# Expert scores of a PEER layer by seven block products: from three quads of expert tiles and six pairs of row blocks to four quads and seven pairs

## The chip, the cores and the metric

The kernel runs on one core of a Trainium2 chip. The metric is the device time of the program in microseconds (us), the median of three runs. The core has a matrix engine (PE), a vector engine (DVE, VectorE), an activation engine (ACT, ScalarE), a general engine (POOL, GpSimd) and queues that start transfers (nearly all of them SP's, SyncE's). Each engine takes its own instructions strictly in order and waits at semaphores for the others, so what is queued behind a waiting instruction waits too.

## The reference

x has 2048 rows of 512 numbers. Three things are added: x itself, the real part of a two-dimensional Fourier transform of the normalised x, and a PEER expert layer with 32 heads, 64 x 64 = 4096 experts and 2 experts chosen per head.

```python
xn = _layernorm(x, axis=-1)
# FNet: a = xn @ Cd^T, b = xn @ Sd^T; y = Cs @ a - Ss @ b
# PEER, with q1, q2 = halves of xn @ w_q[h] and K = 2:
s1 = jnp.einsum("nhd,ed->nhe", q1, k1)
s2 = jnp.einsum("nhd,ed->nhe", q2, k2)
i1 = jnp.argsort(-s1, axis=-1)[..., :K]
i2 = jnp.argsort(-s2, axis=-1)[..., :K]
# the four sums t1 + t2, the best two of them: scores top_s, experts top_e
g = _softmax(top_s, axis=-1)
act = _gelu(jnp.einsum("nd,nhkd->nhk", xf, u[top_e]))
out = jnp.einsum("nhk,nhk,nhkd->nd", g, act, v[top_e])
return x + _A_ref(...) + out
```

## The kernel before, in words

The 2048 rows are 16 row blocks of 128. The 4096 experts are 16 groups of 256. `u_sb[g]` and `v_sb[g]` hold the weights of group g as two f16 numbers each, a high and a low part, and a product of two such pairs is three f16 matmuls (high by high, high by low, low by high).

**Up to 78 us** the kernel normalises x and prepares the Fourier matrices and the folded query-key matrices.

**78 to 418 us, the scores.** Eight chunks j of four heads run over 16 row tiles i; a slot is one (j, i), counted n = 16 j + i. PE computes the scores of a tile (`s_mm`, line 252, 12 matmuls) into one of four PSUM buffers, ACT copies them to one of four SBUF buffers (line 952), and VectorE finds the largest values (MAX8, line 956) and their places (FIND_INDEX8, line 960). After each chunk `routing` turns these into the softmax weights g and the expert numbers, in parts that are queued at slots i = 1, 2 and 4 of the next chunk. It goes to and fro between POOL (lines 885 to 887, 890, 896, 902 and on) and VectorE (lines 888, 889, 894, 895, then the CAST of line 897 and the subtraction of line 898). In the same stretch a hand-written list `todo[n]` hangs other work behind the slots:

- `fill_uv(which, g)`: scales the weights of a group, splits them into high and low (ACT lines 780 and 781, POOL line 782). A table `slots` says where: the u tiles 0, 1, 2 and 3 come at slots 29, 31, 36 and 45.
- `sum_u(g, part)`: for a group that belongs to a quad, part 0 makes four sums of quadrants of the u tile (POOL lines 809 to 812) in a scratch that lies in a v tile not yet filled, called at the end of `fill_uv`; parts 1 and 2 five slots after the fill split them into high and low (`split4`: ACT line 794, POOL line 795) and store them to `s_d` in HBM.
- `sum_x(b, part)`: the same for a pair of row blocks (POOL lines 823, 824 and 829 to 832, then `split4` and a store to `t_d`).
- `m_prep` (POOL line 167, 2 operations a call) and `stage_v` (POOL line 852) prepare other weights.

**418 to 1103 us, the phases.** For each row block b a z phase computes x times u for all 4096 experts and takes gelu of it, and a v phase multiplies the weighted activations by v. The z phases come for two row blocks at once, with two v phases between them, but for blocks 0, 1, 14 and 15, which have single ones. Two ways of doing z exist:

- `u_part` (matmuls on line 1095): the plain product. For a pair of blocks a call is one expert group, 24 matmuls of 256 columns; for one block it is two groups, 48 matmuls of 128 columns.
- `z_pair` with `slot` (matmuls on line 1168): Winograd's seven products in place of eight for a 2 x 2 block matrix, over a *quad* of four expert groups and a pair of row blocks. A slot is one of the seven products, 24 matmuls of 128 columns. Products 1, 2 and 4 read u tiles as they are; 5, 6, 7 and 3 read sums, which `ring_load` (line 1151) brings from `s_d` into a ring of three tiles of 512 KB. After its matmuls a slot hands its PSUM bank to ACT (a copy or gelu) and VectorE (an addition, lines 1204, 1212 and 1216).

In each z pair of before, groups 4 to 15 go in three quads (21 slots), and groups 0 to 3 are plain calls ("c" in the string `SEQ`, which writes the order out by hand).

Beside z and v run, for each row block: `g_mm(b, k)`, k = 0 to 3 (VectorE builds one-hot tiles L and R on lines 1246, 1251 and 1254 in a ring of three; 32 matmuls on line 1256); `w_part(b, k)` (VectorE line 1264, ACT line 1271, VectorE line 1272), which multiplies the activations by these weights; and single units of a comparison of the given Fourier matrices with those that the kernel makes itself (`compare`: VectorE lines 1332, 1338, 1340, 1351 and 1357, ACT line 1377, with loads of 448 KB; `fit`: ACT). A table built with `put(phase, place, ...)` says behind which eighth of a v phase or sixteenth of a z pair each of them is issued: G, W, `compact_d`, U for `compare`, F for `fit`. The v tiles of groups 9 to 15 do not stay on chip and come from `v_d` by transfers of 512 KB.

## Time and profile before

| | |
|---|---|
| median of three runs | 1132.64 us (1132.04 to 1133.97) |
| the profiled execution | 1132.17 us, of which the span that the trace covers is 1130.4 us |
| busy in the span | PE 1114.2, weight loads 724.4, DVE 960.3, ACT 657.5, POOL 319.4 us |
| granted PE clock, mean | 0.998 |
| scores | 78 to 417.7 us |
| phases z(0), z(1), v(0) | 417.7 to 488.7 us |
| phases from z(2, 3) on | 488.7 to 1103 us |

The table is read so: an engine that is busy for nearly the whole span is the one whose work sets the time, unless much of what it does there is waiting under another name. Lines such as L1168 are those of the kernel before.

### The profile page before, as it was taken

The numbers are of one execution on the slowest core, as the hardware profiler recorded it, in microseconds if no ns is written. First come the engines' busy times: TensorE is split into PE (matmuls) and PEld (weight loads), VectorE is DVE, ScalarE is ACT, GpSimd is POOL, SyncE is SP. The second block draws the span as 40 slices with busy tenths as digits, with TensorE's granted clock in tenths as the row PEclk, the third lists the DMA queues.
The fourth block names the chain that finished last, engine by engine and source line by source line (L and its number), as shares of the span: only waits on it lengthen the run. The fifth ranks groups of instructions, "written<-read, shape, count | busy, mean of one in ns | idle before, by whom it ended". The sixth has DMA issues, their size and how long they took to land.

```text
span 1130.4 us, 28284 instructions
## 1 busy us (share of the span) xinstructions
PE 1114.2 (99%) x11180; PEld 724.4 (64%) x11180; DVE 960.3 (85%) x2873; ACT 657.5 (58%) x1099; POOL 319.4 (28%) x357
## 2 busy tenths in 40 slices
...
GB/s 274 289 207 171 162 168 197 112 154 190 105 187 103 104 50 190 157 249 143 258 216 184 239 206 199 235 218 187 226 199 215 227 199 225 190 246 167 239 150 106
DMA packets 122540, 213.10 MB, mean 189 GB/s; under 512 B 34580, under 2 KB 62107, under 8 KB 122398
## 3 DMA queue, kind: packets, MB, share of 16 engines
...
HBM read 178.34 MB, written 27.07 MB: 182 GB/s over the span
## 4 chain that ended last, share of the span: by engine, by line
PE 50%; DVE 10%; DMA 3%; ACT 2%; POOL 2%; issue 1%; SPq 0%; DVEq 0%; ACTq 0%; POOLq 0%
PE v L1301 24%; PE z L1168 13%; PE z L1095 10%; PE g L1256 4%; DMA cx<-in_cb_dram 3%; DVE L L1246 2%; DVE vals L956 1%; DVE idx L960 1%; DVE w L1264 1%; DVE act L1272 1%; DVE cx L1351 1%; DVE R L1251 0%; DMA fit<-in_wq_dram 0%; DVE cx L1340 0%; POOL v L824 0%
## 5 line engine op out<-in xcount | busy, mean ns | idle before, releaser
L252 PE MATMUL s<-m,xq 128*128 128x512 f16 x1344 | 297.4, 379 | 1.0 <-ACT ss L952 0.5
L1301 PE MATMUL v<-v,act 128*128 128x512 f16 x1056 | 233.4, 379 | 1.0 <-DMA v<-v_d 1.0
L252 PEld LDWEIGHTS <-xq 128*128 128x128 f16 x1344 | 129.8, 98 | 152.2 <-issue 2.4
L1314 POOL TENSOR_TENSOR y<-y,xr 128x512 f32<-128x512 f32 x15 | 26.1, 1740 | 623.4 <-DMA y<-y_d 383.7
L1246 DVE TENSOR_TENSOR L<-io_lam,cmp 128x2048 f16<-128x2048 f16 x128 | 157.5, 1230 | 26.9 <-PE g L1256 26.8
L1301 PEld LDWEIGHTS <-act 128*128 128x128 f16 x1056 | 101.2, 98 | 118.7 <-issue 1.3
L1095 PE MATMUL z<-xb,u 128*128 128x128 f16 (+1 forms) x2112 | 154.3, 234 | 0.1
L1095 PEld LDWEIGHTS <-u 128*128 128x128 f16 x2112 | 141.4, 98 | 6.6 <-issue 0.2
L956 DVE MAX8 vals<-ss 128x8 f32<-128x64 f32 x896 | 133.5, 216 | 5.6 <-ACT ss L952 5.6
L1301 PE MATMUL v<-v,w 128*128 128x512 f16 x480 | 106.3, 379 | 0.1
L952 ACT ACTIVATE ss<-s,wsc 128x512 f32<-128x512 f32 x120 | 81.4, 682 | 41.2 <-PE s L252 35.1
L1377 ACT ACTIVATE cx<-cx 128x896 f32<-128x896 f32 x64 | 60.4, 944 | 72.6 <-DVE cx L1357 53.2
L1168 PEld LDWEIGHTS <-s 128*128 128x128 f16 x1656 | 94.8, 98 | 0.1
L960 DVE FIND_INDEX8 idx<-vals,ss 128x8 uint16<-128x256 f32 x224 | 93.8, 419 | 0.0
L1271 ACT ACTIVATE act<-w 128x1024 f16<-128x1024 f32 x36 | 48.3, 1357 | 68.3 <-DVE w L1264 68.0
L1301 PEld LDWEIGHTS <-w 128*128 128x128 f16 x480 | 45.9, 98 | 53.6 <-issue 0.4
L1168 PE MATMUL z<-x,s 128*128 128x128 f16 x1248 | 78.1, 219 | 0.0
L1168 PEld LDWEIGHTS <-u 128*128 128x128 f16 x1296 | 74.9, 98 | 1.8 <-issue 1.4
L1256 PEld LDWEIGHTS <-L 128*128 128x128 f16 x2048 | 60.3, 96 | 12.7 <-issue 2.1
L1351 DVE TENSOR_TENSOR cx<-cx 128x512 f32<-128x512 f32 (+2 forms) x84 | 48.4, 613 | 23.5 <-DMA cx<-in_cb_dram 23.5
L1264 DVE SCALAR_TENSOR_TENSOR w<-act,scl,g 128x1024 f32<-128x1024 f32 x44 | 55.8, 1277 | 10.3 <-ACT act L1195 10.3
L1256 PE MATMUL g<-R,L 128*128 128x32 f16 x2048 | 61.9, 176 | 1.6 <-DVE R L1254 1.5
...
## 6 DMA issues: line engine op xcount, KB each, us to landing
...
```

The source lines that it names most:

```text
L252: nc.tensor.matmul(ps, xt[i][:, l, kd, :], m[:, r, kd, :], start=(n == 0), stop=(n == 3 * KD - 1))
L952: nc.scalar.activation(s, ps, AF.Copy, scale=inv)
L956: nc.vector.max(vals[:, i, w, :, h], s[:, g, :])
L960: nc.vector.max_index(idx[:, i, w].rearrange("p k h -> p (k h)"), vals[:, i, w, 0:2].rearrange("p k h -> p (k h)"), s[:, w * HC:g + 1, :]. ...
L1095: nc.tensor.matmul(ps if n == 1 else ps.rearrange("p (b n) -> p b n", b=2), ug[:, l, c % 2, kd, :], xb2[:, k0, r, kd, :] if n == 1 else xb ...
L1168: nc.tensor.matmul(bank[:, t * P:(t + 1) * P], lt, rt, start=(t == k == 0 and op in "125"), stop=(t == 3 and k == 5), skip_group_check=op ...
L1246: nc.vector.tensor_tensor(L.rearrange("p t (l two) -> p t l two", two=2), io_lam.rearrange("p (l two) -> p l two", two=2).unsqueeze(1).to_ ...
L1256: nc.tensor.matmul(p[:, hf, t * NC:(t + 1) * NC], L[:, t, :], R[:, t, :], start=True, stop=True)
L1264: nc.vector.scalar_tensor_tensor(w, act[:, :, ts], fw, p.rearrange("p h (n c) -> p c (h n)", c=NC), op0=ALU.mult, op1=ALU.mult)
L1301: nc.tensor.matmul(pv, w16[:, c, :, l], v_sb[g][:, r, cc, :], start=(n + cc == 0 and k == 0), stop=(n == 15 and cc == 1 and k == 2))
L1351: nc.vector.tensor_tensor(v, v, tv[:, 0:1].to_broadcast([P, len(ix), 256]), op=o)
L1377: later.append(lambda: nc.scalar.activation(tf[:, P:], tf[:, P:], AF.Abs, accum_out=chk[:, n:n + 1]))
```

## The change

1. `QUADS` gains the quad (0, 1, 2, 3), and `PAIRS` the pair (14, 15). All sixteen expert groups of a z pair go by seven products: `SEQ` has 28 slots and no "c". The single z phases of blocks 14 and 15 become one pair phase.
2. Product 5 no longer takes its sum from the ring. It reads a quarter of the u tile whose own weights no product needs any more (`OPS["5"]` names quarter 2 of `u_sb`), and `first_sum(qd)`, four transfers of 128 KB for each quad, sixteen in all, puts the sums there during v(0). So the ring holds three sums for each quad.
3. The sums of the four new u tiles are made by VectorE, three slots after the fill, in a scratch of their own (slots 32, 34, 39 and 48). Their `split4` and stores follow at the fill's slot + 5, as for the others. `sum_x` for the pair (14, 15) stands at slots 34 and 39.
4. The second `g_mm` for the first block of a pair moves out of the `put` table into `SEQ`, as "g" ahead of the last slot.
5. The `compare` and `fit` units move: four or three `compare` units in a z pair as before, at other places, four in a v phase of an even block (three before), fewer at the end; blocks 14 and 15 lose their single phases and the units in them; G(15, 0), G(15, 1) and `compact_d(15)` find new places.

```diff
-QUADS = (8, 10, 12, 14), (9, 11, 13, 15), (4, 5, 6, 7)
-PAIRS = tuple(range(2, 14, 2))
+QUADS = (0, 1, 2, 3), (8, 10, 12, 14), (9, 11, 13, 15), (4, 5, 6, 7)
+PAIRS = tuple(range(2, NT, 2))
@@ fill_uv
             if which == 0 and not safe and any(g in q for q in QUADS):
                 SRAW[g] = raw
-                sum_u(g, 0)
+                if g > 3:
+                    sum_u(g, 0)
@@ sum_u
-            par = [f for w, f in fills if w == 0 and any(f in q for q in QUADS)].index(g) % 2
-            s4 = scratch(8 - par)
+            par = [f for w, f in fills if w == 0 and f > 3].index(g) % 2 if g > 3 else g % 2
+            s4 = scratch(8 - par if g > 3 else g)
+            hi = v_sb[4 if g in (2, 3) else 6].rearrange("p l c d -> p (l c d)")
+            eng = nc.gpsimd if g > 3 else nc.vector
...
-                nc.gpsimd.tensor_tensor(r[0], a[2], a[3], op=ALU.add)
-                nc.gpsimd.tensor_tensor(r[1], r[0], a[0], op=ALU.subtract)
-                nc.gpsimd.tensor_tensor(r[2], a[0], a[2], op=ALU.subtract)
-                nc.gpsimd.tensor_tensor(r[3], a[1], r[1], op=ALU.subtract)
+                eng.tensor_tensor(r[0], a[2], a[3], op=ALU.add)
+                eng.tensor_tensor(r[1], r[0], a[0], op=ALU.subtract)
+                eng.tensor_tensor(r[2], a[0], a[2], op=ALU.subtract)
+                eng.tensor_tensor(r[3], a[1], r[1], op=ALU.subtract)
@@ the list of slots
+                if g < 4:
+                    todo[n + 3].append(lambda at, g=g: sum_u(g, 0))
                 todo[n + 5].append(lambda at, g=g: (sum_u(g, 1, at), sum_u(g, 2)))
-            for n, b in zip((19, 22, 25, 106, 109, 118), PAIRS):
+            for n, b in zip((19, 22, 25, 106, 109, 118, 34), PAIRS):
                 todo[n].append(lambda at, b=b: sum_x(b, 0, at))
@@ the z pair
-            SEQ = "1a 5a 2a 6a c 3a 1b 7a 2b 5b 4a 6b c 3b 1c 7b 2c 5c 4b 6c c 3c 7c c 4c".split()
+            SEQ = ("1a 5a 2a 6a 3a 1b 7a 2b 5b 4a 6b 3b 1c 7b 2c 5c 4b 6c 3c 1d 7c 2d 5d 4c 6d 3d 7d "
+                   "g 4d").split()
...
-            OPS = {"1": (0, None, None, 0), "2": (1, None, None, 1), "5": (None, 0, 0, None), "6": (None, 1, 1, None),
+            OPS = {"1": (0, None, None, 0), "2": (1, None, None, 1), "5": (2, None, 0, None), "6": (None, 1, 1, None),
+        def first_sum(qd):
+            for t, g in enumerate(QUADS[qd]):
+                nc.sync.dma_start(u_sb[g][:, :, 1, 0:2, :].rearrange("p l k e -> p l (k e)"),
+                                  s_d[qd, 0].rearrange("p (t l f) -> t p l f", t=4, l=2)[t])
@@ the table of phases
-        phases += [("z", 14), ("v", 13), ("z", 15), ("v", 14), ("v", 15)]
+        for b in range(2, NT, 2):
...
+        phases += [("v", 15)]
+            for n in range(4):
+                put(("v", 0), n, lambda qd=3 - n: first_sum(qd))
+        put(("v", 13), 5, G(15, 0))
+        put(("v", 13), 7, G(15, 1))
-                    for cg in (9, 12, 15) if len(ph) == 3 else (0, 2, 3, 6):
+                    for cg in (9, 11, 15) if ph[1] > 2 else (9, 11, 13, 15):
                         put(ph, cg, U)
-                    for cg, f in enumerate((None, F[1], F[1], None, U, U, U, F[0]) if ph[1] % 2 == 0 else (
+                    for cg, f in enumerate((None, F[1], F[1], U, U, U, U, F[0]) if ph[1] % 2 == 0 else (
```

Three places in the order of the instructions follow. The numbers behind the names are those of buffers; a row is line, operation, output, inputs and tile.

The first is POOL in chunk j = 2 of the scores, from the middle of the routing of the chunk before to its last operation there, which multiplies into g. Before (line 896 is that operation, g the softmax weights, w_126 and wh the query weights of `m_prep`, line 782 the low part of u tile 2):

```order
L167 TENSOR_TENSOR w_126<-w_126,wh_2_2009 128x1024
L167 TENSOR_TENSOR w_126<-w_126,wh_3_2097 128x1024
L896 TENSOR_TENSOR g_0_2205<-c_0_2040,g_0_2205 128x16x4
L782 TENSOR_TENSOR u_129<-uv_2_2049,u_129 128x1024
L852 TENSOR_TENSOR uv_10_2154<-uv_10_2154,vh_2291 128x1024
```

With the change (line 899 is the same operation; lines 826 to 835 are `sum_x` of the pair (14, 15), line 796 the low parts of the sums of u tiles 0 and 1):

```order
L167 TENSOR_TENSOR w_126<-w_126,wh_2_2009 128x1024
L826 COPY v_922<-ss_2_2068 128x1
L827 TENSOR_TENSOR v_922<-xq_110 128x1024
L832 TENSOR_TENSOR v_923<-v_922 128x256
L834 TENSOR_TENSOR v_923<-v_922 128x256
L833 TENSOR_TENSOR v_923<-v_922,v_923 128x256
L835 TENSOR_TENSOR v_923<-v_922,v_923 128x256
L796 TENSOR_TENSOR v_915<-v_915,v_921 128x1024
L167 TENSOR_TENSOR w_126<-w_126,wh_3_2101 128x1024
L796 TENSOR_TENSOR v_916<-v_916,v_921 128x1024
L899 TENSOR_TENSOR g_0_2225<-c_0_2044,g_0_2225 128x16x4
L782 TENSOR_TENSOR u_129<-uv_2_2053,u_129 128x1024
```

Eight operations now stand between the two of `m_prep` and ahead of the multiplication: `sum_x` with six, and two low parts.

The second is VectorE at the same place, with the change: the copy of g (line 900, 897 before) waits for POOL's line 899, lines 959 and 963 are MAX8 and FIND_INDEX8 (956 and 960 before), and lines 812 to 815 are the sums of u tile 2.

```order
L900 CAST z<-g_0_2225 128x16x2x4
L963 MAX_INDEX idx_1966<-vals_1965,ss_4_2189 128x8
L901 TENSOR_TENSOR z<-g_0_2225,z 128x16x2x4
L812 TENSOR_TENSOR v_917<-uv_2_2053 128x256
L814 TENSOR_TENSOR v_917<-uv_2_2053 128x256
L813 TENSOR_TENSOR v_917<-v_917,uv_2_2053 128x256
L959 MAX vals_1965<-ss_5_2254 128x8 x5
L963 MAX_INDEX idx_1966<-vals_1965,ss_5_2254 128x8
L959 MAX vals_1965<-ss_5_2254 128x8 x3
L815 TENSOR_TENSOR v_917<-uv_2_2053,v_917 128x256
```

The four sums stand behind the copy and the subtraction of the routing and ahead of the maxima of row tile 5; the sums of u tiles 0 and 1 stand further up, and those of u tile 3 further down.

The third is ACT at the end of the z phase of blocks 4 and 5 (act4 is the activation of block 4, w4 that of block 5, z5 and z1 PSUM banks of products). Before, lines 1102 are gelu of plain calls, line 1195 gelu of a quad, lines 1209 and 1215 copies of products 6 and 7:

```order
L1215 ACTIVATE w4_126<-z1_4_2_8793 128x4x128
L1195 ACTIVATE w4_126<-w4_126,scl_93 128x4x128
L1102 ACTIVATE act4_8366<-z4_3_9130,scl_93 128x256
L1102 ACTIVATE w4_126<-z4_3_9130,scl_93 128x256
L1195 ACTIVATE act4_8366<-z1_4_2_8793,scl_93 128x4x128
```

With the change (lines 1217, 1219 and 1225 are the copies of products 5, 6 and 7, line 1205 gelu):

```order
L1217 ACTIVATE act4_8519<-z5_4_3_9214 128x4x128
L1205 ACTIVATE act4_8519<-z1_4_2_8884,scl_93 128x4x128
L1219 ACTIVATE w4_126<-z1_4_3_9125 128x4x128
L1205 ACTIVATE w4_126<-w4_126,scl_93 128x4x128
L1225 ACTIVATE w4_126<-z1_4_3_9125 128x4x128
L1205 ACTIVATE w4_126<-w4_126,scl_93 128x4x128
L1205 ACTIVATE act4_8519<-z1_4_3_9125,scl_93 128x4x128
```

Between the copy of product 7 and the last gelu of product 4 there were two gelus of a plain call and one of the quad; now there is one gelu, of the other half of block 5.

41 lines of the change are left out of this document (20 added, 21 removed).

## The prediction

> **What bounds the kernel now.** I read the page's busy line first, then the table of windows by stage, then single stretches of the timeline.
>
> ```profile
> span 1130.4 us, 28284 instructions
> PE 1114.2 (99%) x11180; PEld 724.4 (64%) x11180; DVE 960.3 (85%) x2873; ACT 657.5 (58%) x1099; POOL 319.4 (28%) x357
> core 0: us, PE busy (x) PEld busy (x) DVE busy (x) ACT busy (x) POOL busy (x), PEclk, DMA share, GB/s
> 153.00:201.00 48.00, 48.00 (x313) 24.02 (x312) 41.51 (x215) 42.68 (x72) 35.66 (x42) 1.00 0.54 178
> 333.00:378.00 45.00, 45.00 (x293) 21.95 (x292) 41.13 (x216) 33.95 (x52) 40.95 (x46) 1.00 0.39 112
> 378.00:417.70 39.70, 39.06 (x182) 17.54 (x180) 35.41 (x188) 21.15 (x35) 25.45 (x30) 1.00 0.19 65
> 465.00:488.70 23.70, 23.40 (x191) 11.44 (x187) 23.63 (x32) 11.36 (x14) 0.00 (x0) 1.00 0.67 235
> 529.45:574.89 45.44, 45.44 (x355) 22.81 (x353) 43.38 (x79) 20.55 (x30) 2.26 (x1) 1.00 0.67 229
> 661.36:702.73 41.37, 41.18 (x704) 39.97 (x699) 31.98 (x50) 21.94 (x40) 1.32 (x1) 1.00 0.57 202
> ```
>
> In the windows the columns are busy microseconds and instructions of PE, its weight loads, DVE, ACT and POOL, then the granted clock. PE is busy for 1114.2 of 1130.4 us at full clock: fewer PE columns shorten the program wherever the others keep up. They have little in hand. In the scores (153 to 418) VectorE is busy for 41.5 of 48 us in 215 instructions, and what is missing is mostly the gap of some 15 to 30 ns at each; POOL is at 41 of 45 us later. The row 465 to 488.7 is v(0), with VectorE full; 529 to 575 two v phases; 661 to 703 a z pair, where VectorE has 9 us left.
>
> **The change on PE.** Timeline rows: start, duration, engine, line, tile.
>
> ```profile
> 661.36 1.50 PE L1168 MATMUL z<-xb,u 128*128 128x128 f16 x24
> 662.70 1.50 PE L1168 MATMUL z<-x,s 128*128 128x128 f16 x24
> 666.72 2.78 PE L1095 MATMUL z<-xb,u 128*128 128x256 f16 x24
> 669.34 0.95 PE L1256 MATMUL g<-R,L 128*128 128x32 f16 x32
> 670.14 1.50 PE L1168 MATMUL z<-xb,s 128*128 128x128 f16 x24
> 1016.98 10.88 PE L1095 MATMUL z<-xb,u 128*128 128x128 f16 x192
> 1027.70 0.95 PE L1256 MATMUL g<-R,L 128*128 128x32 f16 x32
> ```
>
> Durations overlap the next row, so starts count. A slot takes 662.70 - 661.36 = 1.34 us (24 matmuls, 55.8 ns each), a plain call 669.34 - 666.72 = 2.62, a `g_mm` 670.14 - 669.34 = 0.80. A z pair was 21 x 1.34 + 4 x 2.62 = 38.62 us and becomes 28 x 1.34 = 37.52: -1.10 in each of six pairs, -6.6. Blocks 14 and 15 took 192 matmuls in 1027.70 - 1016.98 = 10.72, so 768 in 42.87, and become 37.52: -5.35. Their `g_mm` and v phases stay. PE's own work: **-12.0 us**. Seven products for eight save an eighth on paper; here a group of experts goes from 2.62 to 37.52 / 16 = 2.35.
>
> [...]
>
> **The change in the scores.** Operations of POOL and VectorE there:
>
> ```profile
> 131.80 2.13 POOL L795 TENSOR_TENSOR v<-v,v 128x1024 f16<-128x1024 f32 x1 [2.09 <-ACT v L794]
> 133.91 0.18 POOL L823 COPY v<-ss 128x1 f32<-128x1 f32 x1
> 134.18 2.12 POOL L824 TENSOR_TENSOR v<-xq 128x1024 f32<-128x1024 f16 x1
> 136.38 0.73 POOL L829 TENSOR_TENSOR v<-v 128x256 f32<-128x256 f32 x1
> 171.82 0.32 POOL L896 TENSOR_TENSOR g<-c,g 128x64 f32<-128x64 f32 x1 [0.31 <-DVE g L895]
> 172.10 2.14 POOL L782 TENSOR_TENSOR u<-uv,u 128x1024 f16<-128x1024 f32 x1
> 172.17 2.15 DVE L897 CAST z<-g 128x128 f16<-128x128 f32 x1
> 174.36 0.29 DVE L898 TENSOR_TENSOR z<-g,z 128x128 f16<-128x128 f32 x1
> 215.40 2.14 POOL L782 TENSOR_TENSOR u<-uv,u 128x1024 f16<-128x1024 f32 x1
> 215.86 1.83 DVE L898 TENSOR_TENSOR z<-g,z 128x128 f16<-128x128 f32 x1
> L780 ACT ACTIVATE v<-uv,ss 128x1024 f16<-128x1024 f32 x9 | 10.3, 1141 | 1.9 <-POOL v L795 1.8
> L1338 DVE TENSOR_TENSOR cx<-cx 128x256 f32<-128x256 f32 x16 | 6.7, 417 | 4.7 <-DMA cx<-in_cb_dram 4.6
> DVE vals L956 <- ACT ss L952: 5.6, 5, 2.0
> 195.47 0.74 DVE L956 MAX8 vals<-ss 128x8 f32<-128x64 f32 x5 [1.02 <-ACT ss L952]
> 198.50 0.74 DVE L956 MAX8 vals<-ss 128x8 f32<-128x64 f32 x5 [0.97 <-ACT ss L952]
> 242.11 0.74 DVE L956 MAX8 vals<-ss 128x8 f32<-128x64 f32 x5 [0.78 <-ACT ss L952]
> DVE pm L888 <- POOL c L887: 12.4, 6, 3.4
> 248.30 0.23 DVE L888 TENSOR_TENSOR pm<-c,c 128x64 f32<-128x64 f32 x1 [2.17 <-POOL c L887]
> 382.40 0.23 DVE L888 TENSOR_TENSOR pm<-c,c 128x64 f32<-128x64 f32 x1 [3.39 <-POOL c L887]
> 409.61 8.23 PE L252 MATMUL s<-m,xq 128*128 128x512 f16 x36 [0.51 <-ACT ss L952]
> ```
>
> The order puts `sum_x` of the new pair (0.18 + 2.12 + 4 x 0.73 = 5.2 us) and two low parts (2 x 2.13) ahead of the POOL operation that multiplies g (L896, the order's L899): 9.5 us. Before, POOL stood idle for only 0.31 us ahead of it, so it comes about **9.5 us** later, and VectorE, whose CAST (L897) needs it, stands with all the MAX8 queued behind. The first two bursts of sums (u tiles 0 and 1) stand ahead of that CAST and cost nothing: VectorE would wait in that time.
>
> The burst for u tile 2 stands behind it: four subtractions or additions of 256 columns, 0.42 us each by L1338. They run while POOL is in 2.1-us operations, and there the trace shows a lock-step: the same L898 took 0.29 us with POOL free but 1.83 when it began 0.46 behind a POOL operation, and both ended within 0.15 us of each other; the CAST did so too (172.17 beside 172.10). [...] Between 4 x 0.34 (issued back to back) and four waits of 1.7 on top I take one and a bit: **3.3 us**; for u tile 3, in a stretch where POOL is busy for 0.74 of the time, likewise but with more of it in POOL's gaps: **1.8**.
>
> Against that VectorE had spare time in the chunk, 1.02 + 0.97 = 2.0: it is 12.6 us late. PE doesn't feel it at once, since four PSUM and four SBUF buffers let it run ahead. Later VectorE wins back what it used to wait: 0.78 at 242, and at L888, where six waits make 12.4 us, the four from 248.30 to 382.40 hold 9.5 of them; each keeps about 1 us for POOL's own three additions, so some 5.4 can go. Together 6.2. **+6.4 us** are left when the scores end, where PE already waits for these copies (0.51 at 409.61), and v(0) behind has VectorE full, so nothing is won back there. Bounds: 9.5 - 2.0 - 6.2 = 1.3 if the bursts fit into gaps; with eight exposed operations at (0.42 + 1.7) = 17 in place of 5.1, 18.
>
> ACT gets one copy for each new split, five of 1.14 us by the like-shaped L780: 5.7 us, in a window where 48 - 42.7 = 5.3 are free. I take 0, because VectorE's delay in the same stretch gives ACT as much; without that cover it is 0.4.
>
> **The ends of z pairs and the v phases.**
>
> ```profile
> L1215 ACT ACTIVATE act<-z 128x512 f32<-128x512 f32 x12 | 7.0, 580 | 0.7 <-PE z L1168 0.7
> L1216 DVE TENSOR_TENSOR act<-act,act 128x512 f32<-128x512 f32 x6 | 4.2, 692 | 4.1 <-ACT act L1215 3.8
> 677.19 1.50 PE L1168 MATMUL z<-x,u 128*128 128x128 f16 x24 [0.19 <-ACT act L1215]
> 1007.43 2.75 PE L1301 MATMUL v<-v,act 128*128 128x512 f16 x12 [1.00 <-DMA v<-v_d]
> ```
>
> Product 4 adds into the bank that ACT copies after product 7 (L1215, 0.58 us). At 677.19 a slot of 1.34 us lay between the two, ACT came to the copy late, and PE waited 0.19. Before, the last pair of the phase had a plain call of 2.62 between; the new end has only the 0.80 of a `g_mm` ("7d g 4d"). Product 7 drains 0.16 after the next may start (1.50 - 1.34), the copy takes 0.58, and the ways between engines some more: about 0.2 over the 0.80. **+1.4** for 7 x 0.2. If "g" waits in its turn (its L and R must come from VectorE ahead of it), or ACT has a gelu in hand, a wait of up to 0.8 each: 5.6; if all is hidden, 0.
>
> VectorE has one more quad in each pair, three additions of 0.69 = 2 us in a window with 9.4 free, and a fourth `compare` unit in even v phases, where the two phases leave 2.1 us (43.38 of 45.44): taken as 0, up to +3 in all. `first_sum` sends 2 MB more in v(0), which has a DMA share of 0.67. Its place is SP's queue, among the 512-KB loads of v tiles: 2 MB at 235 GB/s are 9 us of transfer; a late v tile costs like the 1.00 at 1007.43, up to 3; taken as 0, since a third of the engines' time is free. Ring loads fall from four to three for each quad, so the z pairs read no more than before. Product 5 reads quarters that lie in SBUF, no new wait.
>
> **Sum.** 1132.17 (the profiled run; span 1130.4 and 1.8 around it) - 12.0 + 6.4 + 1.4 = 1128.0; the median lies 0.5 above that run. I forecast 1128, and for this case alone 1123 to 1133.
>
> **Rivals.**
> A. *The delay of the scores eats the gain.* The sums lock step with POOL each time: 1132.2 - 12.0 + 18 + 1.4 = 1139.6, slower. It decides from 12 us of VectorE's delay left at 418 us. For: the pairs 215.40/215.86; POOL at 0.75 to 0.9. Against: the spare waits of 9.5 us. 0.25.
> B. *The scores absorb it.* POOL's chain moves up because its first operations waited before (2.09 at 131.80), or the bursts fall into gaps: 1132.2 - 12.0 + 1.4 = 1121.6. For: PE waits for only 1.0 us in all of the scores. Against: 0.31 idle at L896. 0.17.
> C. *The phases give it back*: 5.6 at z ends and 3 for v: 1132.2 - 12.0 + 6.4 + 8.6 = 1135.2. For: VectorE at 43.4 of 45.4. Against: a wait of only 0.19 in a pair. 0.12.
> D. *The slots don't keep 55.8 ns without plain calls between*: weight loads are 39.97 of 41.37 us in the z window, so the extra 7 x 24 loads of a pair could become the bound. If PEld's share were full, a pair would be 28 x 1.40 = 39.2 in place of 37.52, +1.7 x 7 = 11.8: 1139.8, slower. Against: in 661 to 666 slots follow each other at 1.34. [...] 0.02.
> The forecast has the rest, 0.44.
>
> **How the numbers follow.** 0.2%, 2.3 us, is about what a measurement of this kernel tells from no change. The forecast's case gives 0.31 faster, 0.10 same, 0.03 slower; B 0.17 faster; C 0.03, 0.04, 0.05; A 0.02 same and 0.23 slower; D 0.02 slower. Together 0.51, 0.16, 0.33. The range of 8 in 10 goes from the low side of B, 1118, to A's 1139.
>
> **What would show it.** Right: a z pair some 1 us shorter with slots at 1.34; PE's busy time 12 us less; POOL's L899 about 9 us later than L896 and a wait of VectorE for it; PE waits of some 5 us in sum at the end of the scores; a wait of 0.2 at each last product 4. Wrong: no PE wait in the scores (B), PE waits over 12 us there (A), a wait at "g" or at L1301 in the phases (C), slots over 1.38 (D).

## The result, and the profile after

| | before | after |
|---|---|---|
| median of 6 runs | 1132.86 us (1130.65 to 1133.97) | 1162.43 us (1158.56 to 1166.56) |
| the profiled execution, its span | 1132.17, 1130.4 us | 1159.94, 1157.9 us |
| ratio, 95% interval | | 1.0259 [1.0237, 1.0281] |

The change makes the kernel 2.6% slower. From the page of the changed kernel, its span, busy times, two rows of slices and the chain of waits, and behind them the chain of the kernel before:

```profile
span 1157.9 us, 29155 instructions
...
PE 1113.6 (96%) x11516; PEld 724.6 (63%) x11516; DVE 988.4 (85%) x2919; ACT 681.6 (59%) x1126; POOL 335.7 (29%) x368
...
PE   9999998999999999999999999999989999998997
...
PEclk8999999999999999999999999999999999999999
...
PE 33%; DVE 22%; DMA 9%; POOL 4%; ACT 4%; issue 2%; SPq 1%; POOLq 0%; ACTq 0%; DVEq 0%
```

```profile
PE 50%; DVE 10%; DMA 3%; ACT 2%; POOL 2%; issue 1%; SPq 0%; DVEq 0%; ACTq 0%; POOLq 0%
```

PE was busy for 99% of the span and is now for 96%, and the chain that ended last, half of it PE's before, is a third PE's. Little of PE's own work shows as saved (1114.2 to 1113.6). The clock hides over half of it: in this execution the granted clock was 0.50 at the start for 10.24 us and twice in the phases for 3.41 us, and PE was busy for 2.9 us more up to the first score matmul (22.84, 19.99 before) and for 1.9 and 1.7 us more in two places of the phases, as the windows below show. What PE waited for, in sum, times and longest:

```profile
PE z L1179 <- ACT act L1217: 7.9, 4, 2.4
PE g L1266 <- DVE R L1264: 5.2, 7, 1.2
PE m L148 <- POOL w L167: 4.7, 3, 3.0
PE v L1311 <- DMA v<-v_d: 4.3, 3, 2.3
PE z L1179 <- ACT w L1217: 4.2, 3, 2.1
PE z L1179 <- ACT act L1225: 3.0, 3, 1.3
PE s L252 <- ACT ss L955: 2.6, 5, 1.0
```

L1179 are the slots of the z pairs, L1217 the copy of product 5, L1225 that of product 7, L1266 the `g_mm`, L1311 the v phases. Laid out by stage (from the first matmul of each to that of the next, in the two profiled executions):

| stage | before | after | difference | forecast |
|---|---|---|---|---|
| up to the first score matmul | 22.5 | 25.6 | +3.1 | 0 |
| scores | 395.2 | 402.4 | +7.3 | +6.4 |
| z(0), z(1) | 47.5 | 47.5 | 0 | 0 |
| v(0) | 23.5 | 24.6 | +1.0 | 0 |
| six z pairs | 246.9 | 254.6 | +7.8 | -5.4 |
| six pairs of v phases | 275.2 | 283.1 | +7.9 | 0 |
| from block 14's z on | 119.6 | 119.9 | +0.4 | -5.2 |

The first row is not the change. The kernels below have the same code there and took 21.5 to 25.6 us, by the granted clock: 25.2 to 25.6 where it was 0.50 for 10.24 us, 23.4 to 24.0 where it was so for 6.83 us, at most 22.6 in the others. One window of the start, of the kernel before first and of the change second (columns as in the prediction; the clock is the third number from the end):

```profile
10.60:20.84 10.24, 9.10 (x57) 6.91 (x57) 9.16 (x27) 8.59 (x23) 2.98 (x11) 1.00 0.94 313
```

```profile
10.60:20.84 10.24, 10.24 (x35) 7.66 (x35) 7.80 (x18) 7.67 (x20) 2.41 (x7) 0.50 0.83 307
```

The scores came out near the forecast. The loss is in the phases; two places show it, and a third place shows the scores. The first is z(4, 5), from 587.9 us: rows of PE, ACT and SP (start, duration, engine, line).

```profile
597.41 0.42 SPq L1438 DMA_DIRECT2D fit<-in_wq_dram  x1
600.23 0.72 ACT L1205 ACTIVATE w<-w,scl 128x512 f32<-128x512 f32 x1 [1.38 <-DVE w L1226]
604.02 1.06 ACT L1439 ACTIVATE fit<-fit 128x1024 f32<-128x1024 f32 x1 [3.06 <-DMA fit<-in_wq_dram]
605.07 0.58 ACT L1217 ACTIVATE act<-z 128x512 f32<-128x512 f32 x1
605.70 1.50 PE L1179 MATMUL z<-xb,s 128*128 128x128 f16 x24 [2.12 <-ACT act L1217]
```

A `fit` unit's load was issued at 597.41 and is not there when ACT comes to its activation. ACT stands for 3.06 us, does the unit's work, and only then the copy of product 5 that stands behind it in its order. PE has waited 2.12 us for that copy, since product 3 adds into the same PSUM bank. Six of the seven waits for L1217 have such a stand of ACT ahead of them, 1.8 to 3.5 us at a `fit` unit.

The kernel before has the unit at the same place. In its z pairs from (4, 5) to (12, 13) ACT stood there for only 0.1 to 1.3 us, as in this row of z(6, 7):

```profile
675.51 1.06 ACT L1429 ACTIVATE fit<-fit 128x1024 f32<-128x1024 f32 x1 [1.32 <-DMA fit<-in_wq_dram]
```

In those five pairs the activation began 4.4 to 5.3 us behind the issue of its load before, and 5.7 to 7.5 us with the change. Why the loads come later no run shows. The second place is v(8), first the timeline around a wait of PE, then windows:

```profile
844.20 0.43 SPq L1341 DMA_DIRECT2D cx<-in_cb_dram  x1
844.72 0.38 SPq L1302 DMA_DIRECT2D v<-v_d  x1
850.23 0.58 PE L1311 MATMUL v<-v,w 128*128 128x512 f16 x1 [2.25 <-DMA v<-v_d]
```

```profile
718.50:765.70 47.20, 45.77 (x356) 22.81 (x354) 42.55 (x70) 23.44 (x35) 1.33 (x1) 1.00 0.68 231
807.60:858.80 51.20, 47.69 (x355) 23.28 (x353) 47.48 (x95) 23.33 (x35) 1.43 (x1) 0.97 0.62 213
845.00:850.00 5.00, 2.98 (x14) 1.27 (x13) 3.76 (x6) 1.36 (x1) 0.00 (x0) 1.00 0.91 300
850.00:855.00 5.00, 4.77 (x15) 1.85 (x15) 5.00 (x13) 2.23 (x3) 0.00 (x0) 0.66 0.59 232
858.80:902.90 44.10, 41.87 (x776) 41.71 (x773) 31.75 (x51) 22.91 (x39) 2.44 (x1) 0.96 0.56 189
```

Two v phases (807.6 to 858.8) take 51.2 us in place of 46.8. The loads of v tiles stand on SP's queue between those of the `compare` units and come late by 2.25 us; VectorE is busy for 47.5 us of the 51.2. And then PE is slow: the granted clock is 0.66 on average in the five microseconds behind the wait, 0.50 for 3.41 us of them. So the same two v phases' matmuls keep PE busy for 47.69 us here and for 45.77 in the pair at 718.5, and the z pair behind them (858.8) is at 0.96, with 41.87 us of PE where z(4, 5) at 1.00 has 40.19. That is where part of PE's saved work went. The third place is the scores:

```profile
178.18 2.13 POOL L796 TENSOR_TENSOR v<-v,v 128x1024 f16<-128x1024 f32 x1
182.44 0.20 PE L148 MATMUL m<-sums,w 128*128 128x64 f16 x1 [3.05 <-POOL w L167]
184.43 0.33 POOL L899 TENSOR_TENSOR g<-c,g 128x64 f32<-128x64 f32 x1
184.79 2.13 DVE L900 CAST z<-g 128x128 f16<-128x128 f32 x1 [7.05 <-POOL g L899]
188.87 2.17 POOL L796 TENSOR_TENSOR v<-v,v 128x1024 f16<-128x1024 f32 x1
188.98 2.34 DVE L812 TENSOR_TENSOR v<-uv 128x256 f32<-128x256 f32 x1
191.25 0.41 DVE L814 TENSOR_TENSOR v<-uv 128x256 f32<-128x256 f32 x1
420.01 0.38 PE L252 MATMUL s<-m,xq 128*128 128x512 f16 x1 [0.80 <-ACT ss L955]
```

VectorE waits 7.05 us for POOL's multiplication into g, and the first sum behind it takes 2.34 us where the next takes 0.41: the lock step with POOL, whose L796 ends 0.28 us ahead of it. But PE pays in another place than forecast. Of its waits in the scores 4.7 us are for query weights (L148), between 182 and 232 us, while POOL's L167 stands behind `sum_x`; 1.8 us are for copies of scores (L955) between 197 and 212. At the end of the scores, where the forecast had the loss, they are 0.9 us.

### The profile page after: what moved, and what is told of

It is laid out like the page before. It is cut to its first block, busy times and chain, and to the rows that moved or that the text cites. A ratio compares the mean times of both kernels' runs of the same rounds, so it can differ in the third digit from the quotient of the medians.

```text
span 1157.9 us, 29155 instructions
## 1 busy us (share of the span) xinstructions
PE 1113.6 (96%) x11516; PEld 724.6 (63%) x11516; DVE 988.4 (85%) x2919; ACT 681.6 (59%) x1126; POOL 335.7 (29%) x368
## 4 chain that ended last, share of the span: by engine, by line
PE 33%; DVE 22%; DMA 9%; POOL 4%; ACT 4%; issue 2%; SPq 1%; POOLq 0%; ACTq 0%; DVEq 0%
PE z L1179 16%; PE v L1311 12%; DMA cx<-in_cb_dram 4%; DVE L L1256 4%; DVE w L1274 3%; DVE vals L959 3%; PE z L1100 3%; DMA fit<-in_wq_dram 3%; PE g L1266 3%; DVE idx L963 2%; DVE act L1282 2%; DVE cx L1361 1%; DVE R L1261 1%; DMA v<-v_d 1%; DVE R L1264 1%
## 5 line engine op out<-in xcount | busy, mean ns | idle before, releaser
L1311 PE MATMUL v<-v,act 128*128 128x512 f16 x1056 | 233.6, 379 | 2.0 <-DMA v<-v_d 2.0
L1324 POOL TENSOR_TENSOR y<-y,xr 128x512 f32<-128x512 f32 x15 | 25.6, 1705 | 658.2 <-DMA y<-y_d 353.0
L1311 PEld LDWEIGHTS <-act 128*128 128x128 f16 x1056 | 101.2, 98 | 119.9 <-issue 2.6
L1179 PEld LDWEIGHTS <-u 128*128 128x128 f16 x2688 | 153.9, 98 | 4.0 <-issue 3.4
L1179 PEld LDWEIGHTS <-s 128*128 128x128 f16 x1944 | 111.0, 98 | 12.2 <-issue 12.2
L1311 PE MATMUL v<-v,w 128*128 128x512 f16 x480 | 108.2, 383 | 2.3 <-DMA v<-v_d 2.3
L955 ACT ACTIVATE ss<-s,wsc 128x512 f32<-128x512 f32 x120 | 80.8, 681 | 24.6 <-PE s L252 13.8
L1179 PE MATMUL z<-xb,u 128*128 128x128 f16 x1344 | 85.3, 221 | 0.0
L1179 PE MATMUL z<-x,u 128*128 128x128 f16 x1344 | 81.4, 219 | 3.0 <-ACT act L1225 3.0
L1311 PEld LDWEIGHTS <-w 128*128 128x128 f16 x480 | 46.3, 99 | 56.8 <-issue 4.7
L1179 PE MATMUL z<-x,s 128*128 128x128 f16 x1296 | 81.2, 219 | 0.0
L1205 ACT ACTIVATE act<-act,scl 128x512 f32<-128x512 f32 x56 | 40.1, 720 | 54.9 <-DVE act L1222 28.4
L1266 PEld LDWEIGHTS <-L 128*128 128x128 f16 x2048 | 60.0, 96 | 19.0 <-issue 6.4
L1266 PE MATMUL g<-R,L 128*128 128x32 f16 x2048 | 62.2, 176 | 6.2 <-DVE R L1264 5.2
```

Source lines behind the costliest of these rows:

```text
L955: nc.scalar.activation(s, ps, AF.Copy, scale=inv)
L1179: nc.tensor.matmul(bank[:, t * P:(t + 1) * P], lt, rt, start=(t == k == 0 and op in "125"), stop=(t == 3 and k == 5), skip_group_check=op ...
L1205: nc.scalar.activation(d, d if src is None else src, AF.Gelu_apprx_tanh, scale=zsc)
L1266: nc.tensor.matmul(p[:, hf, t * NC:(t + 1) * NC], L[:, t, :], R[:, t, :], start=True, stop=True)
L1311: nc.tensor.matmul(pv, w16[:, c, :, l], v_sb[g][:, r, cc, :], start=(n + cc == 0 and k == 0), stop=(n == 15 and cc == 1 and k == 2))
```

## The experiments

Times are medians; each ratio is to runs of the kernel before on the same chip at the same time.

| run | median, us | ratio [95%] | scores | six z pairs | six v pairs |
|---|---|---|---|---|---|
| after | 1162.4 | 1.0259 [1.0237, 1.0281] | 402.4 | 254.6 | 283.1 |
| e1_sumx | 1165.3 | 1.0276 [1.0245, 1.0306] | 402.8 | 258.8 | 285.7 |
| e2_fitz | 1160.5 | 1.0243 [1.0207, 1.0280] | 402.4 | 254.2 | 284.1 |
| e3_unitz | 1151.0 | 1.0171 [1.0153, 1.0190] | 402.7 | 251.8 | 276.0 |
| e4_all | 1150.0 | 1.0148 [1.0127, 1.0170] | 402.3 | 256.5 | 276.0 |
| e5_fitout | 1160.0 | 1.0238 [1.0202, 1.0275] | 403.1 | 260.0 | 279.6 |
| e6_poolsum | 1154.3 | 1.0189 [1.0172, 1.0206] | 401.7 | 261.3 | 277.1 |
| e7_sumxlate | 1152.0 | 1.0172 [1.0155, 1.0189] | 403.3 | 255.5 | 275.6 |
| e8_spread | 1158.9 | 1.0216 [1.0183, 1.0249] | 406.0 | 261.3 | 275.6 |
| e9_nounits | 1133.7 | 1.0019 [1.0006, 1.0031] | 403.6 | 241.0 | 277.3 |
| e10_seq | 1141.0 | 1.0093 [1.0066, 1.0119] | 402.2 | 244.6 | 276.7 |
| e11_pair | 1129.5 | 0.9982 [0.9963, 1.0001] | 394.6 | 249.1 | 274.0 |
| e12_sumx28 | 1152.6 | 1.0184 [1.0147, 1.0222] | 401.8 | 257.9 | 275.0 |
| e13_spread | 1149.2 | 1.0140 [1.0115, 1.0164] | 412.8 | 247.8 | 275.5 |
| e14_end | 1154.0 | 1.0153 [1.0128, 1.0178] | 412.0 | 246.2 | 275.5 |
| e15_pairend | 1129.3 | 0.9950 [0.9933, 0.9967] | 394.6 | 249.4 | 275.2 |
| e16_xlate | 1138.9 | 1.0067 [1.0044, 1.0089] | 396.4 | 246.6 | 281.5 |
| e17_xlate3 | 1145.2 | 1.0109 [1.0089, 1.0129] | 394.9 | 246.8 | 287.4 |
| e18_own | 1143.4 | 1.0105 [1.0076, 1.0133] | 396.4 | 245.5 | 283.1 |

The last three columns are microseconds of the one profiled execution of each, whose span lies up to 6 us beside the median. z pairs with one and the same order (e3, e6, e7, e8 and e12) read 251.8 to 261.3 us, in part since the clock falls in one execution and not in another (from 690 to 700 us it is 0.83 on average in e6 and e12, 1.00 in e7 and e8); with the order of e10 they read 244.6 to 247.8 (e10, e13, e14, e16 to e18).

### The first three suspects, one edit each

**e1_sumx**, `sum_x` of the new pair behind the routing:

```diff
-            for n, b in zip((19, 22, 25, 106, 109, 118, 34), PAIRS):
+            for n, b in zip((19, 22, 25, 106, 109, 118, 37), PAIRS):
```

> The change with one edit: sum_x of the pair (14, 15) goes from slots 34 and 39 to 37 and 41, so in POOL's order only one weight operation (2.1 us) and one low part (2.13) stand ahead of the multiplication into g (L899), not sum_x (5.2) and two of each. Theory POOL-chain: of the 8 us that the scores gained, most goes: VectorE's 7.1 us wait for L899 falls below 2, the PE waits in the scores (7.4 us) to about 3, the time by 4 to 6 us, to about 1157. Rival, POOL's load as such: the 5.2 us of sum_x cost the same wherever they stand, the wait moves to another POOL operation, and the time stays within 2 us of 1162.

VectorE's wait for L899 fell to 0.4 us, and the scores didn't change (402.8): the rival, though the median is 3 us above its time. The work came back as one wait for the next chunk's query weights. Timeline row and windows of e1:

```profile
219.37 0.24 PE L148 MATMUL m<-sums,w 128*128 128x64 f16 x1 [3.45 <-POOL w L167]
```

```profile
219.00:224.00 5.00, 4.63 (x31) 2.43 (x32) 5.00 (x25) 3.67 (x6) 3.81 (x6) 0.50 0.20 55
```

The clock is at 0.50 for 5.4 us behind it, until 224.78; half of that, 2.7 us, is an estimate of what PE's matmuls lose there.

**e2_fitz**, the `fit` unit of a z pair at its end:

```diff
-                    put(ph, 8, F[0])
+                    put(ph, 15, F[0])
```

> The change with one edit: the fit unit inside each z pair goes from sixteenth 8 to sixteenth 15. In the trace of the change ACT stands 3 us at the activation of a fit unit whose load has not landed, and the copy of product 5 (L1217), for which PE waits (12 us in seven z pairs), is queued right behind it. Theory fit-ahead-of-copy: the L1217 waits fall from 12 to under 3 us and the time by 8 to 12 us, to about 1152. Rival, ACT waits for VectorE's additions anyway (the gelus L1205 wait 50 us for L1222 and L1226): the copy is as late as before behind a gelu, PE's waits stay at 10 us or more, and the time at 1160 or more.

The time is the rival's, the way to it is neither's. The waits for L1217 are gone from PE's list, and waits for L1219, the copy of product 6, are there (6.9 and 1.9 us). Rows of ACT in z(4, 5) of e2:

```profile
606.09 0.95 ACT L1387 ACTIVATE cx<-cx 128x896 f32<-128x896 f32 x1 [3.06 <-DVE cx L1367]
607.03 0.58 ACT L1219 ACTIVATE w<-z 128x512 f32<-128x512 f32 x1
```

Ahead of this copy ACT stands at a `compare` unit, for 2.2 to 4.2 us where PE waits for product 6. What is shown is that with one unit out of the way ACT stands at the next one.

**e3_unitz**, a `compare` unit from the even v phases to the z pairs:

```diff
-                    for cg in (9, 11, 15) if ph[1] > 2 else (9, 11, 13, 15):
+                    for cg in (9, 11, 13, 15):
-                    ... (None, F[1], F[1], U, U, U, U, F[0]) if ph[1] % 2 == 0 ...
+                    ... (None, F[1], F[1], None, U, U, U, F[0]) if ph[1] % 2 == 0 ...
```

> The change with one edit: the fourth compare unit of the even v phases goes back into the z pairs (four there, three in v). Theory VectorE-load: the v pairs are 8 us longer in sum because VectorE has no room there; a unit less saves 0.5 to 1 us in each of six pairs, the time falls by 3 to 5 us, to 1158. Rival, the queue of transfers: the v phases lose their time where loads of v tiles are issued late behind other entries of SP's queue, a compare unit less in the even ones changes little, and the z pairs lose as much as the v phases win: within 2 us of 1162.

More than the theory's size: the six v pairs are back at 276.0 us (275.2 before), the waits for v tiles fell from 4.3 to 0.7 us, and the time by 11 us. No z pair that took a unit on got longer by more than 0.3 us. So the fourth unit was nearly the v phases' whole loss; whether through VectorE's time or through its loads on SP's queue, the run doesn't tell, since the unit brings both.

**e4_all**, the three edits together.

> The three edits together. If all three theories hold the gains add: 4 to 6, 8 to 12 and 3 to 5 us, so 1139 to 1147. If the rivals hold, 1157 to 1162. If it falls short of the sum of the three single runs by over 3 us, the three share a cause (SP's queue or the granted clock).

Neither range: it is e3 over again, as the single runs say. e1 and e2 only move waits.

### Units, slack and the copies in the z pairs

**e5_fitout**, as e3 with the `fit` units in the v phases (one more of them goes to v(13); its line is not shown).

```diff
-                    put(ph, 8, F[0])
-                    ... (None, F[1], F[1], None, U, U, U, F[0]) ...
+                    ... (None, F[1], F[1], F[0], U, U, U, F[0]) ...
```

> As e3_unitz, and no fit unit inside a z pair: six go to the sixth-free place of the even v phases (where the compare unit was), one to v(13). Theory fit-ahead-of-a-copy (e2 only moved the 3 us stand of ACT from the copy of product 5 to that of product 6): with no fit activation between the copies the waits for L1217 and L1219 (about 10 us in e3's z pairs) fall below 2 us, the z pairs to 40 to 41 us each, the time by 7 to 10 us below e3's 1151, to 1141 to 1144. Rival, the copies are late because of the compare activations (L1387) and gelus that wait for VectorE: the waits stay above 5 us, the time within 3 us of 1151.

The rival, and worse: 1160 us, with z pairs at 260.0. ACT's rows in z(4, 5) of e5:

```profile
607.80 0.95 ACT L1387 ACTIVATE cx<-cx 128x896 f32<-128x896 f32 x1 [4.09 <-DVE cx L1367]
608.75 0.58 ACT L1219 ACTIVATE w<-z 128x512 f32<-128x512 f32 x1
```

With no `fit` there, ACT stands for 4.09 us at the activation of a `compare` unit, whose VectorE part waits for its own load, and the copy of product 6 behind it is late.

**e9_nounits**, as e3 with no unit of either kind in the z pairs. `SKF` and `SKU` stand for a unit that is left out, with constants from POOL for its results; their definition is not shown.

```diff
-                    put(ph, 8, F[0])
+                    put(ph, 8, SKF)
                     for cg in (9, 11, 13, 15):
-                        put(ph, cg, U)
+                        put(ph, cg, SKU)
```

> As e3_unitz, with the compare and fit units inside the seven z pairs left out (28 of 68 compare units and 7 of 35 fit units; the columns they would fill get constants from GpSimd). Theory units ahead of the copies: ACT stands at their activations, which wait for loads and for VectorE, and the copies that PE needs are queued behind; without them the z pairs have no waits but the 0.1 to 0.2 at the last product 4, and take 40 to 40.5 us each in place of 41.5 to 43.4; about 13 us in seven pairs, so 1136 to 1140. Rival, the additions of the quads themselves are too slow for an order without plain calls: the waits at products 3 and 7 stay at 1 us a pair, z pairs 41 us and more, 1145 or more.

The theory, and more than its size: 1133.7. All waits of z slots over 0.3 us are gone. The window of z(4, 5), of e9 first and of the change second:

```profile
583.31:623.34 40.03, 40.03 (x775) 39.99 (x772) 26.85 (x38) 19.49 (x31) 1.40 (x1) 1.00 0.50 156
```

```profile
587.88:630.19 42.31, 40.19 (x775) 40.02 (x771) 31.13 (x49) 22.70 (x39) 1.27 (x1) 1.00 0.57 197
```

40.03 us with PE busy throughout, which is within 0.1 us of the forecast's 37.52 and three `g_mm` of 0.80. Five of the seven pairs read so; z(2, 3) has one `g_mm` less (39.23), and z(10, 11) took 41.65 with the clock at 0.50 for 3.41 us. The change's pair has the same PE work and 2.1 us of waits. The units that are left out must be done somewhere, so this is a measurement and no proposal. It takes away their loads and their work on VectorE and ACT as well as their place in the order.

**e10_seq**, as e3 with the slots in another order, three between most of the products that share a bank (two between 6 and 7 of the first quad, and two or fewer in the last).

```diff
-            SEQ = ("1a 5a 2a 6a 3a 1b 7a 2b 5b 4a 6b 3b 1c 7b 2c 5c 4b 6c 3c 1d 7c 2d 5d 4c 6d 3d 7d "
+            SEQ = ("1a 5a 2a 6a 1b 3a 7a 2b 5b 6b 4a 1c 3b 7b 2c 5c 6c 4b 1d 3c 7c 2d 5d 6d 4c 3d 7d "
                    "g 4d").split()
```

> As e3_unitz, with the slots in another order, so that inside the pair three slots (4.0 us) lie between the products that share a PSUM bank (5 and 3, 6 and 7, 7 and 4) in place of two (2.7); before, with the plain calls, it was up to 5.3. Units stay. Theory slack: the waits behind ACT's copies (13 us in e3) shrink by up to 1.3 us each, to 3 to 6 us in sum, the time to 1141 to 1145. Rival, the waits have another length than the slack (the stands of ACT just grow with it, since its loads are set by the same slots): within 3 us of 1151.

The theory: z pairs from 251.8 to 244.6 us and the time to 1141.0, with all units in place. PE's list has no wait for an ACT copy of products 5, 6 or 7 any more; what is left is 4.7 us for VectorE's additions (L1222). ACT's stands at the `fit` units of z(4, 5) to z(12, 13) shrank as well, to 0.5 to 1.9 us. So both are needed for the loss: units that stand ahead of the copies, and only 2.7 us between products.

**e11_pair**, the seventh pair alone, groups 0 to 3 plain. Of its edit the list of quads and the order of slots are shown (`c` is a plain slot); what goes with them, such as the dropped sums of u and the `g_mm` put back, is not.

```diff
-QUADS = (0, 1, 2, 3), (8, 10, 12, 14), (9, 11, 13, 15), (4, 5, 6, 7)
+QUADS = (8, 10, 12, 14), (9, 11, 13, 15), (4, 5, 6, 7)
+            SEQ = "1a 5a 2a 6a c 3a 1b 7a 2b 5b 4a 6b c 3b 1c 7b 2c 5c 4b 6c c 3c 7c c 4c".split()
```

> One part of the change alone: blocks 14 and 15 as a seventh pair (with e3's places of the units and sum_x at slots 34 and 39), but groups 0 to 3 stay plain calls between the slots, with three quads, no sums of u by VectorE and no first_sum. Theory slack: z pairs are at 41.0 to 41.4 us as before and show no waits over 0.5; the end is 3 to 5 us shorter than before's 119.6; the scores lose 3 to 5 us to sum_x: 1129 to 1134. Rival, units and loads are the cause and not the slack: the z pairs lose 1 us each here too, 1137 or more.

The theory's time, and its mechanism in the main: the waits for L1217 are gone, and the longest wait left in the z pairs is 0.8 us for L1225 (3.0 us in sum). Its parts came out otherwise. The z pairs took 41.1 to 42.0 us, the end 119.2 in place of 119.6, no gain there in the profiled execution, and the scores lose nothing (394.6). 0.9982 [0.9963, 1.0001] is not clear of no change.

### The 7 us of the scores

VectorE's delay was read in each kernel as the time from the first score matmul to the first maximum of chunk 3, less before's 184.0 us. The two rows of before's timeline, and the two of the change's:

```profile
22.49 1.89 PE L252 MATMUL s<-m,xq 128*128 128x512 f16 x8 [0.32 <-DVE m L227]
206.45 0.35 DVE L956 MAX8 vals<-ss 128x8 f32<-128x64 f32 x2
```

```profile
25.63 1.67 PE L252 MATMUL s<-m,xq 128*128 128x512 f16 x7
222.09 0.35 DVE L959 MAX8 vals<-ss 128x8 f32<-128x64 f32 x2
```

It is 196.5 - 184.0 = 12.5 us in the change, and 7.2 are left at the start of chunk 7. In e1 it is 11.0 at chunk 3, though the wait for L899 is gone. Five more runs tried its parts.

**e6_poolsum**, as e3 with the sums of u by POOL:

```diff
-            eng = nc.gpsimd if g > 3 else nc.vector
+            eng = nc.gpsimd
```

> As e3_unitz, with the sums of u tiles 0 to 3 made by POOL at the same slots in place of VectorE. Theory POOL's load sets the loss in the scores (7.3 us there in the change, unmoved by e1): POOL gets 16 x 0.73 = 11.7 us more, the scores lose 3 to 10 us more, and the time goes to 1154 to 1161. Rival, VectorE's sums in lock step with POOL are the loss (the prediction's 5 us): the scores win 3 to 5 us, the time goes to 1146 to 1148.

**e7_sumxlate** and **e8_spread**, `sum_x` of the new pair at slot 112, and in e8 the low parts four slots later too:

```diff
-            for n, b in zip((19, 22, 25, 106, 109, 118, 34), PAIRS):
+            for n, b in zip((19, 22, 25, 106, 109, 118, 112), PAIRS):
-                todo[n + 5].append(lambda at, g=g: (sum_u(g, 1, at), sum_u(g, 2)))
+                todo[n + (9 if g < 4 else 5)].append(lambda at, g=g: (sum_u(g, 1, at), sum_u(g, 2)))
```

> As e3_unitz, with sum_x of the pair (14, 15) at slots 112 and 116, where POOL is busy for 25 of 40 us, out of chunks 2 and 3 altogether. Theory POOL's load in chunks 2 and 3: 7.3 us of 15.9 go from there, PE's waits of 7.3 us in the scores fall to 2 to 4, the time by 3 to 6 us, to 1145 to 1148; some of it may come back at the end of the scores. Rival, VectorE's sums: the time stays within 2 us of 1151.

> As e7_sumxlate, and the low parts of the sums of u tiles 0 to 3 come nine slots after the fill in place of five, so that POOL's order up to the multiplication into g (L899) is that of before. Theory POOL's chain: PE's waits in the scores fall to 1 to 2 us, the time 1 to 3 us below e7. Rival, VectorE's sums: VectorE's 16 additions and their lock step (5 us) remain, PE's waits for the copies of scores stay at 3 us or more, the time within 1 us of e7.

**e12_sumx28**, `sum_x` ahead of the routing (28 in place of 34), and **e13_spread**, as e10 with the low parts of u tiles 0 to 3 one a chunk:

```diff
-                todo[n + 5].append(lambda at, g=g: (sum_u(g, 1, at), sum_u(g, 2)))
+                todo[(n + 5, 56 + 16 * g)[g < 4]].append(lambda at, g=g: (sum_u(g, 1, at), sum_u(g, 2)))
```

> As e3_unitz, with sum_x of the pair (14, 15) at slots 28 and 33, ahead of the routing. e7 showed that with sum_x gone from chunks 2 and 3 PE waits there for only 1.1 us, and e1, e6 and e7 that it costs 5 us again where POOL has a routing to serve. Theory place of sum_x: ahead of the routing it fills POOL's spare time of chunk 1 (18 of 73 us), the scores take 396 to 398 us from their first matmul in place of 402.7, the time 1145 to 1147. Rival, POOL has no spare time that an operation in order can use: 400 us or more in the scores, within 2 us of 1151.

> As e10_seq, with the low parts and stores of the sums of u tiles 0 to 3 spread out, one a chunk (slots 56, 72, 88, 104 in place of 34, 36, 41, 50); VectorE still makes the sums at slots 32 to 48 and sum_x of (14, 15) stays at 34. e11 (sum_x there, no sums of u) took 394.6 us from the first score matmul to z, e7 (sums and low parts, no sum_x there) waited only 1.1 us in chunks 2 and 3, both together lose 7. Theory POOL's load in two chunks: 8.5 us of POOL's work leave them, the waits for L167 (4.5 us) and for the copies go, the scores take 395 to 397 us in place of 402.3, v(0), which began with VectorE late (27.2 us), 24 to 25: 8 to 10 us, 1131 to 1133. Rival, VectorE's 16 sums are what sum_x cannot stand beside: the scores stay at 400 or more, 1138 to 1142.

None helped. e6 is the same within a microsecond (401.7, and a delay of 11.2 us at chunk 3), though 16 operations went from VectorE to POOL: neither theory. e7's delay at chunk 3 is 6.5 us and is down to 0.4 at chunk 7, then PE waits 4.5 us near the end, where `sum_x` now is:

```profile
407.63 0.58 PE L252 MATMUL s<-m,xq 128*128 128x512 f16 x1 [4.49 <-ACT ss L955]
```

That gives the rival's time for e7. e8 has 9.6 us at chunk 3, 406.0 us of scores and a time 7 us above e7's: neither of its theories. e12 delays chunk 3 by 11.8 us: the rival. In e13 the delay is 10 us at chunk 3 and grows by 1.3 to 2.3 in each of the four chunks after it, which have one low part of 2.13 us each, and the scores take 412.8 us: worse than both. Why nothing is won back there isn't shown. Together with e11 (`sum_x` without the sums of u: 1.6 us, all won back) this suggests a budget: 5 to 6 us of delay are won back until the end, `sum_x` fits or the sums fit, not both.

**e16_xlate** and **e17_xlate3** test that: as e10 with e14's edit, `sum_x` of the new pair (e17: of three pairs) not in the scores but in the v phase ahead of its z pair, made by POOL from the loaded blocks into `x4`. The body of `late_x` and e17's other places for it are not shown.

```diff
-            for n, b in zip((19, 22, 25, 106, 109, 118, 34), PAIRS):
+            for n, b in zip((19, 22, 25, 106, 109, 118), PAIRS):
+            put(("v", 12), 3, late_x)
```

> As e10_seq with e14's move in v(14), and sum_x of the pair (14, 15) not in the scores at all: POOL makes it in v(12) from the loaded blocks straight into x4, where POOL has nothing else to do. The traces so far give VectorE's delay at the start of chunk 3 as 12.5 us with sums of u and sum_x, 6.5 with the sums of u alone, 1.6 with sum_x alone, and 6 us are won back by chunk 7. Theory one budget: 6.5 us of delay are won back, the scores take 395 to 397 us from the first score matmul to z (402 in e10), v(0) 24 to 25 (27.2 in e10): 8 to 10 us below e10's 1141, 1131 to 1133. Rival, the low parts cost again at the end of the scores as in e13: 400 or more, 1138 or more.

> As e16_xlate, with sum_x of the pairs (10, 11) and (12, 13) moved in the same way, out of slots 109 and 118 into v(8) and v(10). Theory one budget: POOL is free at the end of the scores, VectorE's delay is fully gone, PE's wait there (0.8 us) too, and v(0) is at 23.5: 1 to 3 us below e16, 1129 to 1132. Rival: v(8) and v(10) are where VectorE is fullest, POOL's two-input operations lock step with it there and the v phases lose what the scores win: the same as e16 or up to 3 us more.

The budget holds: 396.4 us and 394.9 us in the scores. But the v phases that take it lose as much or more: v(12) of e16 lasts 29.4 us in place of 23.1, v(8) of e17 32.3 in place of some 24. So e16 has its rival's time but not the rival's cause, and e17 is above both theories. Rows of POOL, VectorE and PE in v(12) of e16:

```profile
995.65 2.29 POOL L1571 TENSOR_TENSOR sx<-xb 128x1024 f32<-128x1024 f16 x1 [59.28 <-DVE wr L1397]
995.88 2.07 DVE L1398 TENSOR_TENSOR wr<-wr,w 1x1 f32<-1x1 f32 x1
1003.52 1.24 DVE L1361 TENSOR_TENSOR cx<-cx 128x512 f32<-128x512 f32 x1 [2.15 <-DMA cx<-in_cb_dram]
1008.02 0.24 PE L1266 MATMUL g<-R,L 128*128 128x32 f16 x3 [3.36 <-DVE R L1264]
```

VectorE's subtraction of one number in one partition takes 2.07 us, 0.14 in the change, and ends within 0.01 us of POOL's. Later VectorE stands for loads of `compare` units, and PE waits 3.36 us for R; the granted clock is 0.50 for 6.83 us from 1007.17 on. The wait and half of the 6.83 us make 6.8 by estimate, near the 6.3 us that v(12) loses.

**e18_own** asked whether it was the buffers that `late_x` takes (the working set in `x4` itself, one buffer of the ring in place of two), and put it two places later.

```diff
-            f, t4 = [bp.tile([P, 2 * D], F32, tag="w", name=f"sx{k}", bufs=WB) for k in range(2)]
+            f = x4.rearrange("p l o k n -> p (l o k n)").bitcast(F32)
+            t4 = bp.tile([P, 2 * D], F32, tag="w", name="sx", bufs=WB)
-            put(("v", 12), 3, late_x)
+            put(("v", 12), 5, late_x)
```

> As e16_xlate, and the late sum_x of the pair (14, 15) works in x4 itself and one buffer of the ring of four that w and the compare units use, in place of two, and comes two places later in v(12). Theory: e16's v(12) took 29.4 us in place of 23.1 because two of the four buffers were held, so the loads of the compare units came late and VectorE with the R of the next one-hot product (3.4 us of PE wait and the clock after it); with one buffer it takes 23 to 25, the time 1133 to 1135, still not below before's 1132. Rival: VectorE's lock step with POOL's 2.1-us operations is the cause, v(12) stays at 28 or more, the time at 1138 or more.

v(12) lasts 29.3 us again, but the wait in it is another (4.3 us for a v tile in place of 3.4 for R). The theory fell; the rival's time is right, its mechanism isn't shown. Why the move of `sum_x` makes v(12) late stays open.

### The end, and the version that beats both

**e14_end** (as e13) and **e15_pairend** (as e11), in v(14):

```diff
-                put(ph, 0, G(b + 1, 2))
-                put(ph, 3, G(b + 1, 3))
+                put(ph, 0 if b < 14 else 1, G(b + 1, 2))
+                put(ph, 3 if b < 14 else 4, G(b + 1, 3))
```

> As e13_spread, and in v(14) the third and fourth one-hot products for block 15 come one place later (1 and 4 in place of 0 and 3), where PE waits 1.1 and 0.85 us for VectorE's R in all kernels of the change. Theory: these 2 us go, v(14) takes 23 us in place of 24.85, the time 1 to 2 us less than e13. Rival: the wait moves to the multiplication w that needs the product, no change.

> As e11_pair (seventh pair alone, plain calls kept), with the same move in v(14): 1 to 2 us less than e11's 1129.5, so 1127.5 to 1128.5, below before's by 3 to 4. Rival as for e14: no change.

v(14) went from 24.84 to 24.14 us in e14 (whose time is lost elsewhere: a wait of 3.6 us in v(0)) and from 24.53 to 23.34 in e15. e15 takes 1129.3 us where the kernel before took 1134.2 on the same chip: 0.9950 [0.9933, 0.9967]. The seventh pair without the fourth quad, with e3's places of the units and this move, is 0.5% faster than the kernel before. By stage the gain is at the end, 116.3 us in place of 119.6.

## Why the prediction was wrong, by its steps

- **PE's work, -12.0: right within 1 us.** e9 has z pairs of 40.03 us against 41.02, and the pair of blocks 14 and 15 at 40.03 too, where the two single phases took 23.85 and 23.05 with two `g_mm` (1.6 us) that now stand in v(13). Slots stayed at 1.34 us, 55.8 ns a matmul, so rival D is out.
- **The scores, +6.4: near in size, by another path.** POOL's multiplication came 9.5 us later, as forecast (184.43 against 171.82, each from its first score matmul). VectorE was forecast 12.6 us late and was 12.5; 6.4 were to be left and 7.2 were. The lock step of a later sum stands in the rows 188.87 to 191.25. But the parts of the sum don't add: without the wait for L899 (e1) 11.0 us of delay remain, without VectorE's sums (e6) 11.2. And PE was to feel the delay at the end, through the copies, where it waited 0.9 us; it lost 4.7 us to query weights behind `sum_x` on POOL, a wait that the forecast doesn't name. That the size fits is in part luck. One reading was wrong besides: the 6.5 us that VectorE lacks in the window 153 to 201 are not a gap of 15 to 30 ns at each instruction. Seven waits make 5.9 of them, 2.43 the longest.
- **The ends of z pairs, +1.4, at most 5.6: this step failed.** It took one dependence into account, product 7 to 4 at the end, and gelu as the only thing ahead of the copy. PE's waits were 12.1 us for the copy of product 5 and 3.0 for that of product 7, and the six z pairs took 7.8 us more where 5.4 less were forecast. What the prediction did not see is that the plain calls were the slack of every quad: product 5 to 3 and 6 to 7 had up to 5.3 us between them and now have 2.7, and ACT's order has units there whose loads land 5.7 to 7.5 us behind their issue. e9 (units away) and e10 (slack back) each remove these waits. That the loads were also later than before (4.4 to 5.3 us) adds to it; no run separates the two.
- **VectorE and transfers in the phases, 0, up to +3: failed in size.** The row of 43.38 us busy of 45.44 was quoted, and a fourth `compare` unit was put at nothing all the same. The six pairs of v phases took 7.9 us more, of which e3, without it, wins 7.1 back. The units of two dropped phases had to go somewhere; the end, forecast to win 5.2, paid its own part with waits for R in v(14) (24.9 us in place of 22.4).
- **No term had the clock.** A wait was priced at its length. Behind waits in v(8) and z(10, 11) stand clocks of 0.97 and 0.96 over 95 us, with 3.6 us more of PE time (47.69 and 41.87 us in place of 45.77 and 40.19).

Rival C, "the phases give it back" with a chance of 0.12, is nearest to what happened, at a price of 8.6 where it was some 29: PE's -12.0 became +17.1 from v(0) on (1.0, 7.8, 7.9 and 0.4). And the phases are not the whole of it. In e9, where the six z pairs win 5.9 us and the end 3.4, the scores (+8.4), v(0) (+1.6) and the v phases (+2.1) take more than that, and its ratio is 1.0019. There the delay of the scores eats most of the gain, as in rival A, though with less than A's 12 us.
